# Two attention and two MLP layers on one core: a float32 first block, weights split in streaming slots, a rank for every operation, and four-tile attention steps

## The chip, the core and the metric

The kernel runs on one core of a Trainium2 chip. Its compute engines are PE (TensorE, matrix products), DVE (VectorE), ACT (ScalarE) and POOL (GpSimd); SP issues most of the transfers. The metric is the device time of one execution in microseconds, lower is better. Each number given for a kernel is the median of its runs.

## The reference

Four layers over 2048 tokens of 512 channels, in float32: attention, MLP mixer, attention, MLP mixer, each with layer norms and a residual.

```python
def _A_ref(x, wqkv, wo):            # H = 32 heads of Dh = 16; W, dil = 8, 2
    qkv = (x @ wqkv).reshape(B, S, 3, H, Dh)
    idx = pos[:, None] - off[None, :]                # off = arange(8) * 2
    logits = einsum("bhsd,bhswd->bhsw", q, k[idx]) * Dh ** -0.5
    attn = softmax(where(idx >= 0, logits, -1e9))
    o = einsum("bhsw,bhswd->bhsd", attn, v[idx])
    return o.reshape(B, S, D) @ wo

def _B_ref(x, w1, w2, w3, w4):
    h = gelu(layernorm(x) @ w1)                      # D x D
    # the four quarters of h's channels move by +1, -1, +2, -2 tokens
    x1 = x + shifted(h) @ w2
    return x1 + gelu(layernorm(x1) @ w3) @ w4        # 512 -> 1792 -> 512

x = x + _A_ref(layernorm(x), A_wqkv, A_wo)
x = x + _B_ref(layernorm(x), B_w1, B_w2, B_w3, B_w4)
x = x + _A_ref(layernorm(x), A_wqkv, A_wo)
x = x + _B_ref(layernorm(x), B_w1, B_w2, B_w3, B_w4)
```

## The kernel before

**Tiles and stages.** Tokens are cut into four blocks of 512, each block into four tiles of 128 tokens (one token per partition; even and odd tokens lie on the two halves of the partitions, so that the window's step of two is a step of one). Two layers of four blocks give eight passes n = 0 to 7. Each goes through five stages: `p1_stream(n)` (layer norm, transposes, q, K, V; `p1_quarters` for n = 0), `p2(n)` (attention, in four units of eight heads called quarters), `p3(n)` (wo, residual, norm, w1, gelu), `p4(n)` (shift, w2, residual, norm) and `p5(n)` (the MLP in 14 chunks of 128 hidden channels). Group n of `p4` and `p5` has three or four tiles, five in the last pass, because the shift needs the neighbouring block.

**Numbers.** A float32 operand is split into two float16 parts, hi and lo, after scaling by a power of two; a product is three float16 matmuls (`HLS`, hi*hi, hi*lo, lo*hi). So every weight goes through: load, sum of squares on ACT, a small matmul and a power on POOL that give the scale (`power_of`), hi on ACT, lo on DVE (`rest`). wqkv is split in two parts, q = 0 for the first quarter's columns and q = 1 for the others; `small_weight` does wo, w1 and w2; `big_pair(c)` takes two chunks of w3 and w4 at once through one of the large buffers nT or h, and writes the halves to DRAM (`w34_d`), from where `p5` reads them in every pass into the `w` places.

**Attention.** `p1_quarters` writes q, K and V of one quarter of block 0 straight into the q and kv places; eight transfers then shift K and V by one and two partitions, so that seven earlier tokens stand beside each. `p1_stream` writes q, K and V to DRAM, and each quarter of `p2` loads a window from there. A quarter works on two tiles at a time (`for i in (0, 2)`): multiply K by q (`prod`), sum over the head's 16 channels into `L`; then for all four tiles maximum, subtract, exp (ACT), sum, reciprocal, scale; then again two tiles at a time multiply V by the weights and add the eight window places in three additions. For n = 0 (`PE_SUMS = 1`) PE sums the products by 16 float32 matmuls with the identity per pair of tiles instead, which also transposes the result; `prod0` is a second product buffer for n = 0, which is afterwards lent out as two x and two f32 places (`LENT`).

**Order.** Nothing is emitted in the order of the code. `Graph` collects 3,000-odd operations with their buffers' cells; `plan` is a list scheduler that gives every engine, at each moment of an estimated time, the ready operation with the lowest key whose buffers have a free place, and so fixes each engine's order and each buffer's place. On the chip each engine runs its operations in that order and waits on semaphores. An operation's key is that of its stage, `n - 1.0` for p3 and so on, and `SHIFT` adds a correction by stage, pass and engine:

```python
key += sum(SHIFT.get(k, 0) for k in {(s, None, None), (s, None, e), (s, n, None), (s, n, e)})
```

The word "lock" marks DVE operations that the planner keeps apart from POOL's. Places: mm and acc (4 + 4 PSUM banks), x (9, later 11), f32 (6, later 8), kv (3), q, prod, L, o, ev, nT, h, g and w (8). At the start 64 matmuls on ones (`WARM`) run before any data has come.

## Time and profile before

| | |
|---|---|
| median of 3 runs | 1235.77 us (1235.09 to 1235.9) |
| the profiled execution, its own time | 1236.35 us |
| its span, first to last instruction | 1234.6 us |
| mean granted clock of PE | 0.983 |
| instructions | 16,935 |
| bytes moved by DMA | 175.22 MB, mean 142 GB/s |
| ACT table loads | 56, 71.8 us in all |

In the profile, L252 is the line of the helper that issues every instruction, so groups are told apart by their tiles: `out<-in`, numbers of buffers left out. A matmul row has the duration of one matmul from its first to its last cycle; matmuls overlap, so their cost to PE is the distance between their starts. In a view by time a row is a run of equal instructions with start, duration and count, and in brackets the idle time before it and what ended that. `SPq` rows are issues of transfers, and "granted clock" is the share of its full clock that PE had.

### The profile page before, as it was taken

How to read it: one execution, taken by the hardware profiler on the slowest of the kernel's cores; microseconds unless marked ns; L12 is line 12 of the kernel's file. 1: busy time of each engine (PE TensorE's matmuls, PEld its weight loads, DVE VectorE, ACT ScalarE, POOL GpSimd, SP SyncE). 2: the span in 40 equal slices, each digit the busy share in tenths (PEclk: the TensorE clock that was granted, in tenths of full speed). 3: DMA queues.
4: the chain of work that ended last, by engine and by line, in shares of the span. 5: the costliest groups of instructions: out<-in, count | busy, mean ns of one | idle time of the engine just before them, and what ended most of it. 6: DMA issues, size and time to landing. Idle time of an engine off the chain costs nothing.

```text
span 1234.6 us, 16935 instructions
## 1 busy us (share of the span) xinstructions
PE 1187.9 (96%) x6048; PEld 604.3 (49%) x6048; DVE 929.2 (75%) x1168; ACT 680.7 (55%) x1217; POOL 363.0 (29%) x512
## 2 busy tenths in 40 slices
PE   7799599999999999999999999999999999999997
PEld 5365364455454455444444445444444444444554
DVE  4787689988888999999887988798867898322011
ACT  6775566664655457545653656465556454344332
POOL 4230313412531146023621353135003441232100
PEclk9799799999999999999999999999999999999999
DMA  8546785576536543754347545743457344112321
GB/s 260 183 125 208 208 260 163 126 216 180 142 95 183 153 141 99 175 141 124 90 138 195 140 107 139 192 128 92 128 138 201 98 133 153 61 43 73 107 85 52
DMA packets 119556, 175.22 MB, mean 142 GB/s; under 512 B 11184, under 2 KB 61840, under 8 KB 119472
## 3 DMA queue, kind: packets, MB, share of 16 engines
q1 hardware_dynamic: 117440, 172.65, 49.6%
q10 hardware_dynamic: 2032, 1.50, 0.4%
q8 instruction: 47, 0.77, 0.3%
q14 instruction: 37, 0.30, 0.1%
HBM read 132.64 MB, written 37.87 MB: 138 GB/s over the span
## 4 chain that ended last, share of the span: by engine, by line
PE 85%; DMA 5%; ACT 4%; DVE 2%; SPq 1%; issue 1%; POOL 0%; DVEq 0%; ACTq 0%; POOLq 0%
PE mm L252 63%; PE acc L252 22%; DMA kv<-kv 2%; SPq L252 1%; DMA kv_d<-ev 1%; DVE L L252 1%; DMA w<-in_A_x_dram 1%; ACT g L252 1%; ACT junk L252 1%; DVE prod L252 1%; DMA h<-in_B_w_dram 0%; DMA nT<-in_B_w_dram 0%; DMA w<-g 0%; DMA q_d<-ev 0%; ACT kv L252 0%
## 5 line engine op out<-in xcount | busy, mean ns | idle before, releaser
L252 PE MATMUL acc<-w,g 128*128 128x512 f16 x1302 | 299.3, 379 | 0.0
L252 PE MATMUL mm<-nT,w 128*128 128x512 f16 (+1 forms) x1344 | 294.9, 373 | 0.0
L252 ACT ACTIVATE mm<-mm,s_w 128x512 f32<-128x512 f32 (+2 forms) x158 | 98.3, 623 | 253.3 <-PE mm L252 252.9
L252 PEld LDWEIGHTS <-g 128*128 128x128 f16 x1494 | 148.2, 99 | 167.3 <-issue 15.1
L252 PE MATMUL mm<-wq_hl,xt 128*128 128x512 f16 x1008 | 225.7, 379 | 0.4 <-ACT ev L252 0.3
L252 PEld LDWEIGHTS <-w 128*128 128x128 f16 x1512 | 141.0, 98 | 147.0
L252 DVE TENSOR_TENSOR prod<-kv,q 128x2048 f32<-128x2048 f32 x64 | 149.2, 2333 | 30.7 <-DMA kv<-kv 17.0
L252 PEld LDWEIGHTS <-xt 128*128 128x128 f16 x1008 | 98.6, 98 | 112.0 <-issue 0.7
L252 DVE TENSOR_TENSOR prod<-kv,L 128x2048 f32<-128x2048 f32 x64 | 148.8, 2330 | 0.9
L252 DVE TENSOR_REDUCE L<-prod 128x128 f32<-128x2048 f32 x64 | 145.7, 2279 | 0.6
L252 POOL TENSOR_TENSOR g<-f,g 128x512 f16<-128x512 f32 (+1 forms) x39 | 56.0, 1435 | 278.7 <-ACT f L252 271.6
L252 DVE TENSOR_TENSOR prod<-prod 128x1024 f32<-128x1024 f32 (+1 forms) x113 | 118.3, 1047 | 2.5
L252 PE MATMUL mm<-nT,w_hl 128*128 128x512 f16 x384 | 88.3, 379 | 0.4 <-ACT nT L252 0.2
L252 PE MATMUL mm<-wo_hl,oT 128*128 128x512 f16 x384 | 84.5, 379 | 0.0
L252 PE MATMUL mm<-w_hl,h 128*128 128x512 f16 x384 | 84.5, 379 | 0.0
L252 ACT ACT_TABLE_LOAD x56 | 71.8, 1283 | 19.1 <-PE mm L252 13.1
L252 DVE SCALAR_TENSOR_TENSOR g<-mm,c_g,g 128x512 f16<-128x512 f32 (+1 forms) x56 | 40.9, 729 | 48.7 <-ACT g L252 48.6
L252 ACT ACTIVATE g<-mm,c_g 128x512 f16<-128x512 f32 (+1 forms) x112 | 75.0, 672 | 3.3
L252 ACT ACTIVATE ev<-mm,s_kv 128x128 f32<-128x128 f32 x112 | 46.8, 470 | 54.1 <-PE mm L252 42.5
L252 POOL COPY h<-h 128x126 f16<-128x126 f16 (+3 forms) x56 | 43.1, 793 | 104.3 <-DVE h L252 101.5
L252 POOL TENSOR_TENSOR g<-prod,g 128x512 f16<-128x512 f32 (+1 forms) x17 | 25.4, 1496 | 151.8 <-ACT prod L252 151.8
L252 PEld LDWEIGHTS <-oT 128*128 128x128 f16 x426 | 41.6, 98 | 49.7
(183 smaller groups left out, 1424.9 us busy)
## 6 DMA issues: line engine op xcount, KB each, us to landing
w<-w SPq DMA_DIRECT2D x224, 256.0 KB
kv<-kv_d SPq DMA_DIRECT2D x112, 352.0 KB
kv_d<-ev SPq DMA_DIRECT2D x112, 128.0 KB
q_d<-ev SPq DMA_DIRECT2D x28, 256.0 KB
w<-g SPq DMA_DIRECT2D x28, 256.0 KB
q<-q_d SPq DMA_DIRECT2D x28, 256.0 KB
x<-x SPq DMA_DIRECT2D x27, 256.0 KB
w<-in_A_x_dram SPq DMA_DIRECT2D x32, 128.0 KB
```

What stands on the lines that cost most here:

```text
L252: i = f(*a, **k).ins
```

## The change

What it does, part by part:

- **Order.** `SHIFT` goes. `PLACES` gives each of the 3,029 operations, in the order in which the code makes them, a rank from 0 to 3,028, and that rank is its key.
- **Block 0 in float32.** `p1_quarters` turns the tiles into float32 (`turn_f32`) and multiplies them by the raw wqkv: four float32 matmuls of 384 columns per tile and quarter (for the first quarter 256 and 128). Quarters 1 to 3 are written to x places; from there one transfer each copies K and V into kv places, beside the shifts. In `p5(0)` (`PLAIN = 1`) w3 and w4 are loaded in float32 and used unsplit: per chunk 4 matmuls up, one gelu, 3 matmuls down. In the trace of before these were 12 and 9 in float16.
- **Splitting.** wqkv is split as a whole after block 0's products, with one scale; its evictions need one instruction instead of two. `hi` may go to ACT or POOL (`hi_of`), squares of wqkv to ACT or DVE. `big_pair` stages each of its four pieces in a `w` place. Loads of x of blocks 1 to 3 and of all weights but wqkv wait for the eviction of quarter 0's last q and K (`begun`).
- **Attention.** A quarter's four tiles go through the multiply, the sum over channels, the multiply by V and each addition in one instruction. `L` is laid out head, tile, window place, so that maxima and sums run over neighbours. `PE_SUMS` goes: block 0 adds on DVE and transposes like the others. `prod` is one buffer of four tiles; `prod0` and its lent places go (x 9, f32 6).
- **Norms.** The small instruction that made minus the mean goes; ACT's square takes the sum by its scale and bias.
- **Last pass.** In `p5(7)` all lo parts are made on DVE, and each part of a group has its own `down`.

```diff
-        key += sum(SHIFT.get(k, 0) for k in {(s, None, None), (s, None, e), (s, n, None), (s, n, e)})
-        o.key, o.alts, o.succ, o.n, o.est = key, alts, [], 0, 0.0
+        o.key, o.alts, o.succ, o.n, o.est = PLACES[len(self.ops)], alts, [], 0, 0.0
...
-        "x": places("x", X_OWN, [P, D], F32, const, part[:2]),
+        "x": places("x", 9, [P, D], F32),
-        "prod": places("prod", 1, [P, 2 * W * P], F32),
-        "prod0": places("prod0", 1, [P, 2 * W * P], F32),
+        "prod": places("prod", 1, [P, NT * W * P], F32),
-        "f32": places("f32", F_OWN, [P, D], F32, const, part[2:]),
+        "f32": places("f32", 6, [P, D], F32),
...
+    def turn_f32(key, n, dst, cell, out):
+
+        ps = Buf("mm")
+
+        def fn():
+            for c in range(NC):
+                f = slice(P * c, P * (c + 1))
+                T.transpose(ps.t[:, f], n.t[:, f], ident)
+        pe(key, 0.44, fn, [n], [ps, (dst, "new")])
+        act(key, 0.6, lambda: A.activation(out(), ps.t.rearrange("p (c t) -> p c t", c=NC), AF.Copy), [ps], cell)
...
+            q, kv = first_q[qt] = (Buf("x"), [Buf("x"), Buf("x")]) if qt else (Buf("q"), [Buf("kv"), Buf("kv")])
+            first = 0 if qt else PAD * P
...
+                for ks in ((0, 1), (2,)) if qt == 0 else ((0, 1, 2),):
...
+                        for c in range(NC):
+                            rhs = src_of(0, c) if f0 == 0 else src_of(1, c)[:, :, f0 - P:f0]
+                            T.matmul(o, f32v(xts[i].t, D)[:, P * c:P * (c + 1)], rhs[:, ks[0]:ks[0] + n],
+                                     start=(c == 0), stop=(c == NC - 1))
...
+                    if qt == 0 and i == NT - 1 and ks[0] == 0:
+                        begun = [done]
...
+                if qt:
+                    first_q["copied"] = dma(k1, lambda j=j, kv=kv: kv[j].t[:, PAD * P:], lambda j=j, src=src: src[j].t,
+                                        [(src[j], tiles)], [(kv[j], ("own", 0)), (kv[j], "new")], 0.8)
...
+        first = dve(kd + 0.05, 4.46, lambda pv4=pv4, q=q, kv=kv: V.tensor_tensor(
+            pv4(), win(kv[0].t, 0, NT),
+            q.t.rearrange("p (t f) -> p t f", t=NT).unsqueeze(2).to_broadcast([P, NT, W, P]), ALU.mult),
+            q_in + kv_in[0], [pr, (L, "new")], lock=True)
+        dve(kd + 0.04, 4.41, lambda pv4=pv4, Lv=Lv: V.tensor_reduce(
+            Lv(), pv4().rearrange("p t j (h d) -> p t j h d", d=DH), AX.X, ALU.add), [pr], [L])
...
+        dve(kd + 0.02, 4.46, lambda pv4=pv4, Lv=Lv, kv=kv: V.tensor_tensor(
+            pv4().rearrange("p t j (h d) -> p t j h d", d=DH), win_h(kv[1].t, 0, NT),
+            Lv().unsqueeze(4).to_broadcast([P, NT, W, H8, DH]), ALU.mult),
+            [all_L, *kv_in[1]], [pr, (o, "new")], lock=True)
...
-    VEC_G = (0, 2, 4, 6, 8, 10, 12)
+    PLAIN = 1
+    VEC_G = [2] * 7 + [1]
...
+        def up():
+            for k in range(NC):
+                T.matmul(ps.t[:, :P * K], f32v(w3.t, D)[:, P * k:P * (k + 1)],
+                         f32v(nT.t, NC * D)[:, D * k:D * k + P * K], start=(k == 0), stop=(k == NC - 1))
+
+        def down():
+            for k in range(K):
+                T.matmul(acc[k].t, f32v(g.t, D)[:, P * k:P * (k + 1)], f32v(w4.t, D),
+                         start=(c == 0), stop=(c == NF - 1))
...
-    p1_quarters()
     p2(0)
```

More of the change, by code (lines that the diff above doesn't have):

```diff
@@ L283, in __getitem__ @@
             return self.made[j]
-    X_OWN, F_OWN = 9, 6
-    part = [lambda j=j: slots["prod0"][0][:, D * j:D * (j + 1)] for j in range(4)]
-    LENT = [("x", X_OWN), ("x", X_OWN + 1), ("f32", F_OWN), ("f32", F_OWN + 1)]
     slots = {
@@ L491, in stage_of @@
         return (stage0, c) if q == 0 else (stage1[c // 2], c % 2)
-    ssq = [keep(f"ssq{q}", [P, NC]) for q in range(2)]
-    inv_q = [keep(f"inv_q{q}", [P, 1]) for q in range(2)]
     K0 = -9.0
@@ L640, in tile_mixer @@
[L640 removed]
+            [], [stage_of(1, c)], 1.9)
     SC = 3
@@ L834, in p1_stream @@
                                 "p (q f) -> p q f", q=4), [ev], [(kvb[l], qts(par, j - 1))], 0.6)
+    begun = p1_quarters()
+    for i in range(NT):
+        load_x(1, i, K0 + 1.0, begun)
+    op.stage = ("wqkv", 0)
+    ssq, inv_q = keep("ssq", [P, 2 * NC]), keep("inv_q", [P, 1])
+    for q in range(2):
+        for c in range(NC):
+            n = 3 * (P if q == 0 else D - P)
+            dst, acc = [lambda q=q, c=c: part(0, c, q).bitcast(BF16),
+                        lambda q=q, c=c: ssq.t[:, NC * q + c:NC * q + c + 1]]
+            op(-4.0, [(ACT, 0.3 + n * 0.00078, lambda q=q, c=c, dst=dst, acc=acc: A.activation(
+                dst(), src_of(q, c), AF.Square, accum_out=acc()), None),
+                      (DVE, 0.06 + n * 0.00137, lambda q=q, c=c, dst=dst, acc=acc: V.scalar_tensor_tensor(
+                dst(), src_of(q, c), 1.0, src_of(q, c), ALU.mult, ALU.mult, accum_out=acc()), "lock")],
+                [stage_of(q, c)], [(wq, (q, 0, c)), (ssq, (q, c))])
```

547 lines of the change are left out of this document (245 added, 302 removed), and 139 rows, old and new, of tables (PLACES, SHIFT).

## The prediction

> **What bounds the kernel now.** I read the busy shares first, then the span cut into stretches.
>
> ```profile
> PE 1187.9 (96%) x6048; PEld 604.3 (49%) x6048; DVE 929.2 (75%) x1168; ACT 680.7 (55%) x1217; POOL 363.0 (29%) x512
> ...
> 10.36:54.00 43.64, 29.02 (x137) 16.36 (x136) 26.91 (x55) 33.06 (x76) 7.85 (x17) 0.80 0.74 228
> 54.00:165.00 111.00, 90.97 (x556) 61.78 (x554) 83.84 (x117) 69.10 (x151) 28.93 (x38) 0.91 0.63 186
> 165.00:240.00 75.00, 71.64 (x365) 36.44 (x364) 68.66 (x100) 50.56 (x95) 26.06 (x36) 1.00 0.64 181
> 240.00:1200.00 960.00, 958.73 (x4769) 468.24 (x4768) 739.84 (x877) 515.06 (x874) 289.03 (x382) 1.00 0.48 132
> 1200.00:1234.60 34.60, 28.21 (x167) 14.01 (x165) 6.34 (x12) 9.39 (x18) 2.31 (x2) 0.95 0.17 57
> ```
>
> In a stretch the first number behind its bounds is its length, then busy PE, PEld, DVE, ACT, POOL, the granted clock and the DMA share. From 240 to 1200 us PE lacks 1.3 us: an edit there gains only if it takes work from PE. Length minus busy gives PE's gaps: 14.6, 20.0, 3.4, 1.3 and 6.4 us, of 46.7 in all (1234.6 - 1187.9); the first 10.36 us, mostly warm-up, have the other 1.0. The last 6.4 are output transfers; 38 us lie before 240, where the granted clock is 0.80 and 0.91 too. So I asked whom PE waited for (us in all, times, longest), and where (start, duration, count, in brackets the wait before).
>
> ```profile
> PE mm L252 <- ACT f L252: 14.0, 7, 7.8
> PE mm L252 <- DVE mx L252: 6.2, 1, 6.2
> ```
>
> ```profile
> 67.33 3.73 PE L252 MATMUL mm<-ident,prod 128*128 128x128 f32 x32
> 70.90 5.34 PE L252 MATMUL mm<-wq_hl,xt 128*128 128x512 f16 x24
> 76.08 2.11 PE L252 MATMUL mm<-wq_hl,g 128*128 128x384 f16 x12
> ...
> 79.73 2.11 PE L252 MATMUL mm<-wq_hl,g 128*128 128x384 f16 x12
> 81.68 0.60 PE L252 MATMUL mm<-ident,f 128*128 128x128 f32 x4
> 82.11 2.11 PE L252 MATMUL mm<-wq_hl,g 128*128 128x384 f16 x12
> ...
> 144.56 1.12 PE L252 MATMUL mm<-ident,f 128*128 128x128 f32 x4 [7.83 <-ACT f L252]
> ...
> 155.09 5.89 PE L252 MATMUL mm<-ident,prod 128*128 128x128 f32 x32 [6.16 <-DVE mx L252]
> ```
>
> The two largest gaps are bracketed. ACT, late at 144, had itself waited 9.6 us for a pair of MLP weights to land in its one big staging buffer; the gap at 155 is a power step of the same pairs:
>
> ```profile
> 141.93 1.06 ACT L252 ACTIVATE g<-h 128x1024 bf16<-128x1024 f32 x1 [9.62 <-DMA h<-in_B_w_dram]
> ```
>
> **The change part by part.** *PE's work.* Starts of groups give pitches: (76.08-70.90)/24 = 0.216 us for an f16 matmul of 512 columns, (81.68-79.73)/12 = 0.1625 for 384, (70.90-67.33)/32 = 0.1116 for one f32 record of 128, and 82.11-81.68 = 0.43 for four transposes. An f32 matmul leaves two records, so it costs 0.223 for 128 columns, which is four times an f16 column (0.1625 x 4/3 = 0.217). I price f32 at four f16 matmuls of its width: 0.65 for 384, 0.863 for 512; scaling the 128-column row gives 0.67 and 0.893 as the upper end.
>
> ```profile
> L252 PE MATMUL mm<-ident,prod 128*128 128x128 f32 x324 | 42.3, 285 | 7.3 <-DVE mx L252 6.2 <-ACT kv L252 1.1
> ```
>
> By the code, block 0's qkv has 16 x 12 = 192 f16 matmuls of 384 (31.2 us), which become 16 x 4 in f32 (41.6): +10.4. Its MLP up: 14 x 12 = 168 f16 (27.3) become 14 x 4 = 56 f32 (36.4): +9.1. Its down: 14 x 9 = 126 f16 of 512 (27.2) become 42 f32 (36.2): +9.0. Out go the 128 sums of products on PE (256 of the 324 records; the other 68 are transposes from lent places): -28.6. In come 16 transposes: +1.7. Net +1.6, at the upper f32 price +5.3. So PE gains no work and loses none: what the change is worth must come out of gaps and slow clock.
>
> *The beginning, 10 to 54 us.*
>
> ```profile
> 10.36 0.60 PE L252 MATMUL mm<-ident,f 128*128 128x128 f32 x4
> ...
> 11.29 0.58 ACT L252 ACTIVATE g<-mm 128x512 f16<-128x512 f32 x1
> ...
> 15.71 0.82 PE L252 MATMUL mm<-ident,f 128*128 128x128 f32 x4 [2.22 <-POOL f L252]
> 16.33 9.52 PE L252 MATMUL mm<-wq_hl,g 128*128 128x384 f16 x48
> ...
> 29.23 6.34 SPq L252 DMA_DIRECT2D kv<-kv  x8
> ...
> 31.74 7.61 DMA kv<-kv
> ```
>
> The first tile is turned at 10.36, but its products wait for the split of the weights until 16.33. In f32 they need only the turned copy (0.6 of ACT) and the raw weights: start near 12. Sixteen units of 2.6 us then run to about 54, because quarters 1 to 3 go to x places and no longer wait for the kv places that the attention holds. Row 52.60 below shows the streaming products starting at 52.6 already, so the split of wqkv, moved behind, is ready then if ACT and DVE keep their present pace. The gap of 14.6 should fall to 3; bounds 1 (ACT's copy alone) and 14.6. The split's squares and scalings stay on ACT, DVE and POOL, beside 42 us of PE work.
>
> ```profile
> 52.60 5.34 PE L252 MATMUL mm<-wq_hl,xt 128*128 128x512 f16 x24
> ```
>
> *Attention of block 0, 54 to 165 us.* Durations of one instruction on DVE:
>
> ```profile
> L252 DVE TENSOR_TENSOR prod<-kv,q 128x2048 f32<-128x2048 f32 x64 | 149.2, 2333 | 30.7 <-DMA kv<-kv 17.0 <-DMA kv<-kv_d 7.9 <-PE mm L252 5.5
> L252 DVE TENSOR_REDUCE L<-prod 128x128 f32<-128x2048 f32 x64 | 145.7, 2279 | 0.6
> L252 DVE TENSOR_TENSOR prod<-prod 128x1024 f32<-128x1024 f32 x56 | 74.4, 1329 | 0.6
> L252 DVE TENSOR_TENSOR prod<-prod 128x512 f32<-128x512 f32 x57 | 43.9, 771 | 1.9
> L252 DVE TENSOR_REDUCE mx<-L 128x32 f32<-128x256 f32 x64 | 39.0, 610 | 13.0 <-ACT L L252 12.6
> L252 DVE TENSOR_TENSOR L<-L,mx 128x256 f32<-128x256 f32 x64 | 29.2, 457 | 2.2
> L252 DVE TENSOR_TENSOR o<-prod 128x256 f32<-128x256 f32 x56 | 25.1, 449 | 1.9
> L252 DVE SCALAR_TENSOR_TENSOR g<-h,inv_p,g 128x512 f16<-128x512 f32 x16 | 11.1, 746 | 1.5 <-ACT g L252 1.5
> ```
>
> A quarter costs 2 x (2.333+2.333+2.279) + 2 x (1.329+0.771+0.449) + 2 x (0.610+0.457): 21.1 us. Four tiles at once double the width: from 1024 to 2048 columns the time grows by 1.004, so 4096 takes about 4.34 where two took 4.66; the three wide steps and three adds save some 1.7 us, 47 over the 28 quarters that already ran on DVE. The other layout of L I price at nothing, between -0.5 (contiguous maxima and sums) and +0.5 (scattered writes). Before 1200 this is under PE and earns nothing, as do the small scalings of the sums that go.
>
> For block 0, DVE's four quarters (4 x 19.4 = 78, the adds now included) start when the shifted K and V have landed. Landing took 7.61 us at 31.74 (a step of the chain of waits); quarter 0 is now done near 22, so 30. Beside them DVE splits wqkv (12 times 512 columns at 0.746: 9 us), wo, w1, w2 (9 more) and the turned tiles of the streams (12, 9 more): last output at 135, and with all 28 splits of the MLP weights in front (21) at 156. PE's work that needs no attention: 54 + 12 tiles x (36 x 0.216 + 0.43) = 152. So the gap here lies between 0 and 4 us for this chain alone; layer norms of block 0 without other work add a few. Of the present 20.0 us, 14.0 (7.83 + 6.16) hang on MLP weight pairs, which are first needed by block 1 now and stage in eight small w places. I take 8 left; bounds 0 and 20.
>
> *Slow clock.* Busy time by what the granted clock lacks is 29.0 x 0.20 + 91.0 x 0.09 = 14 us at most; directly, the 48 matmuls at 16.33 took 9.52 for 48 x 0.1625 = 7.8, the 32 records at 155.09 5.89 where those at 67.33 took 3.73. Fewer gaps, less of it: I take 8 of the 14 as gained, bounds 0 and 12. The Trainium skill, "TensorE: Matmul & The Clock Gate" (Part 1), says that an idle window of about 3.4 us halves the clock and as long a busy one restores it; the rows behind both long gaps agree (1.12 for 0.60 at 144.56, 5.89 for 3.73 at 155.09), and by that rule alone nearly all 14 would be gained, 6 us more than I take.
>
> *Places and order.* x and f32 lose two lent places each. 17 transposes used the f32 ones (68/4); were each delayed by one 0.75 us step, 13 us; I take 2 (PE has other work), bounds 0 and 13. The float32 MLP reads as many bytes as the split one. SP gets six more copies of K and V (0.8 us each by row 29.23), while PE works on streams. The loads of x of block 1, of wo, w1, w2 and of the MLP weights now wait for quarter 0's last q and K eviction near 22, and the shifts of K and V share their queue; the first user of that x is a stream near 54, 30 us later, against one landing of 7.6 us: nothing, and 7.6 once without that cover. `scale` steps, single evictions and the all-DVE last block shorten covered work: nothing.
>
> *Sum.* 1234.6 + 1.6 (PE) - 11.6 (beginning) - 12 (54 to 165) - 8 (clock) + 2 (places) = 1206.6 of span. Around it lay 1236.35 - 1234.6 = 1.75 us; the profiled execution was 0.6 above the median of 1235.77. So 1207.7; I say 1207.
>
> **The rivals.** *A: everything fills.* Gaps at their lower bounds (1, 0), clock 12, no cost of places: 1234.6+1.6-13.6-20-12+1.2 = 1192. For it: 152 us of independent work against 135. Against: a static order meets late transfers.
>
> *B: DVE's chain decides block 0.* All MLP splits come first and the K and V transfers slip by 8 us in each of three quarters: output at 156 + 24 = 180 against 152, a gap of 28 instead of 8: 1228. For it, DVE's 17 us of waits on kv<-kv; against, three kv places let a pair load ahead.
>
> *C: the longer lock, slower than before.*
>
> ```profile
> 64.94 2.29 DVE L252 TENSOR_TENSOR prod<-kv,q 128x2048 f32<-128x2048 f32 x1 [1.25 <-PE mm L252]
> 65.49 1.80 POOL L252 TENSOR_SCALAR a<-a 128x1 f32<-128x1 f32 x1 [1.16 <-ACT junk L252]
> 68.37 0.19 POOL L252 TENSOR_SCALAR a<-a 128x1 f32<-128x1 f32 x1
> 68.64 0.55 POOL L252 TENSOR_TENSOR a<-a,nhalf 128x1 f32<-128x1 f32 x1
> ...
> 69.29 0.26 POOL L252 TENSOR_SCALAR a<-a,a 128x1 f32<-128x1 f32 x1
> ...
> L252 POOL TENSOR_TENSOR a<-a,nhalf 128x1 f32<-128x1 f32 x32 | 25.0, 782 | 3.2 <-DVE a L252 0.8
> L252 POOL TENSOR_SCALAR a<-a,a 128x1 f32<-128x1 f32 x32 | 21.2, 664 | 3.2
> ```
>
> POOL's 0.19 us step at 65.49 ends only with DVE's multiply. With a multiply of 4.4 us such a wait doubles, about +0.64 us for each of 96 layer norm chains (the last two steps take 0.782 + 0.664 in the mean and 0.55 + 0.26 undisturbed): 61 us if PE stood still for each, 1269; more than 44 of 96 must be exposed to lose what I forecast. If six in ten are, 1245. Against it: PE lacks 1.3 us in 960. The Trainium skill, "SBUF — State Buffer" (SBUF: two separate sides), states this lock for a DVE operation with two SBUF inputs against a GpSimd one that reads SBUF, for the whole instruction; the row agrees.
>
> *D: the change does not do what it says.* The table gives only precedence among ready operations; if the real order of transfers leaves PE as idle as before, 1234.6 + 1.6 + 2 - 2 + 1.2: 1237.
>
> **How the numbers follow.** Forecast 0.52 (1198 to 1217), A 0.14, B 0.18, C 0.10, D 0.06. About 0.2% (2.5 us) is what a measurement of this kernel can tell from no change. The range 1190 to 1233 holds forecast, A and B; C and D lie above. Faster: 0.52+0.14+0.18 and a little of D, 0.85; same: 0.05; slower: C, 0.10.
>
> **What would show it.** The first qkv matmul near 12 and the streams near 54; PE busy about 1181 with the same steady stretch; DVE multiplies of 4.35 us; gaps before 240 near 14. Wrong would be: a PE gap over 10 us, between 100 and 200 us, before wo (B); gaps after 240 released by POOL or ACT f (C); an f32 pitch of 512 above 0.9 us.

## The result, and the profile after

The changed kernel takes 1240.79 us (median of 8 runs, 1238.06 to 1245.12), the kernel before 1235.84 beside it (8 runs, 1234.47 to 1239.03): ratio 1.0039, 95% interval 1.0022 to 1.0057. It is slower by 0.4%; forecast was 1207. The profiled execution took 1240.41 us, its span is 1238.3.

The busy line of the page and the same stretches as before (length, then busy PE, PEld, DVE, ACT, POOL, granted clock, DMA share, GB/s):

```profile
PE 1193.5 (96%) x5676; PEld 592.2 (48%) x5676; DVE 903.5 (73%) x896; ACT 632.0 (51%) x1108; POOL 372.4 (30%) x516
```

```profile
10.36:54.00 43.64, 40.75 (x179) 27.84 (x178) 25.60 (x33) 26.73 (x77) 19.20 (x24) 1.00 0.61 194
54.00:165.00 111.00, 88.69 (x385) 41.62 (x384) 88.75 (x88) 57.75 (x119) 25.90 (x37) 0.91 0.65 174
165.00:240.00 75.00, 69.83 (x322) 35.32 (x320) 70.70 (x80) 50.64 (x94) 31.23 (x44) 0.95 0.69 198
240.00:1200.00 960.00, 951.15 (x4542) 463.26 (x4540) 707.24 (x676) 486.37 (x798) 287.47 (x374) 1.00 0.49 135
1200.00:1238.30 38.30, 33.78 (x201) 16.86 (x198) 7.48 (x13) 7.60 (x16) 0.00 (x0) 0.97 0.23 69
```

Length minus busy gives PE's gaps, to set beside those of the prediction. The prediction gave its 2 us for lost places no stretch; the forecast column has them in the steady one, from 240 to 1200. The last column is a kernel found in the experiments (e11_wide_between); most of its rows are shown there.

| us | before | forecast | after | e11 |
|---|---|---|---|---|
| gap 10.36 to 54 | 14.6 | 3 | 2.9 | 1.5 |
| gap 54 to 165 | 20.0 | 8 | 22.3 | 12.1 |
| gap 165 to 240 | 3.4 | 3.4 | 5.2 | 5.8 |
| gap 240 to 1200 | 1.3 | 3.3 | 8.9 | 1.1 |
| gap after 1200 | 6.4 | 6.4 | 4.5 | 4.5 |
| PE busy | 1187.9 | 1181.5 | 1193.5 | 1186.6 |
| span | 1234.6 | 1206.6 | 1238.3 | 1212.6 |

The opening gained its 11.7 us. The rest of the table took them back: +2.3 from 54 to 165, +1.8 up to 240, +7.6 in the steady stretch, +5.6 of PE's busy time, -1.9 at the end. Together +3.7. The traces split the 5.6: PE was busy for 22.0 us under a granted clock of 0.50 before and for 27.5 us after. Counting half of such time as lost gives 11.0 and 13.7 us, so 2.7 are clock and the other 2.9 work; e11, with the same matmuls, has 8.1 and thus 1.6 of work, as forecast. The rows of PE by time (start, duration, count, in brackets the wait before):

```profile
12.21 1.16 PE L358 MATMUL mm<-nT,g 128*128 128x128 f32 x8 [0.69 <-ACT g L358]
...
53.76 10.52 PE L358 MATMUL mm<-wq_hl,xt 128*128 128x512 f16 x48
...
87.69 5.03 PE L358 MATMUL mm<-wq_hl,xt 128*128 128x512 f16 x12 [4.22 <-ACT ev L358]
...
137.98 1.12 PE L358 MATMUL mm<-ident,f 128*128 128x128 f32 x4 [4.77 <-ACT f L358]
...
172.87 2.75 PE L358 MATMUL mm<-wo_hl,oT 128*128 128x512 f16 x12
...
241.35 2.74 PE L358 MATMUL acc<-w,g 128*128 128x512 f32 x6
243.92 2.74 PE L358 MATMUL mm<-nT,w 128*128 128x384 f32 x8
246.50 0.60 PE L358 MATMUL mm<-ident,o 128*128 128x128 f32 x4
```

The first float32 product starts at 12.21 and the streams at 53.76, as forecast; 2.57/3 = 0.857 and 2.58/4 = 0.645 us bear out the float32 prices of 0.863 and 0.65. But the row at 87.69 waits 4.22 us for an eviction of ACT and takes 5.03 us where 12 matmuls of the same width take 2.75 at 172.87. ACT stood as well. Two of its rows, and the issue of SP that the second waited for:

```profile
76.30 0.69 ACT L358 ACTIVATE ev<-mm,s_q 128x512 f32<-128x512 f32 x1 [5.97 <-DMA kv_d<-ev]
...
86.34 0.63 ACT L358 ACTIVATE junk<-w 128x512 bf16<-128x512 f32 x1 [7.20 <-DMA w<-in_B_w_dram]
```

```profile
80.55 0.73 SPq L358 DMA_DIRECT2D w<-in_B_w_dram  x1
```

The piece for which ACT stands from 79 on is issued at 80.55. And the sums of PE's waits (us, times, longest), where before ACT's f led with 14.0:

```profile
PE mm L358 <- ACT ev L358: 16.5, 8, 4.2
PE mm L358 <- ACT f L358: 16.0, 9, 4.8
```

So transfers were late; the first question was whether SP issued them late, whether they landed late, or whether something else (the 4.4 us steps of DVE) held everything.

### The profile page after: what moved, and what is told of

It is laid out like the page before. It is cut to its first block, busy times and chain, and to the rows that moved or that the text cites. A ratio compares the mean times of both kernels' runs of the same rounds, so it can differ in the third digit from the quotient of the medians.

```text
span 1238.3 us, 15802 instructions
## 1 busy us (share of the span) xinstructions
PE 1193.5 (96%) x5676; PEld 592.2 (48%) x5676; DVE 903.5 (73%) x896; ACT 632.0 (51%) x1108; POOL 372.4 (30%) x516
## 4 chain that ended last, share of the span: by engine, by line
PE 76%; DVE 7%; DMA 7%; ACT 3%; POOL 2%; SPq 2%; issue 2%; ACTq 0%; DVEq 0%; POOLq 0%
PE mm L358 54%; PE acc L358 22%; DVE prod L358 3%; SPq L358 2%; DMA kv<-kv_d 2%; DMA kv<-x 1%; DVE L L358 1%; POOL b L358 1%; DMA w<-in_A_x_dram 1%; POOL a L358 1%; DMA h<-in_B_w_dram 1%; ACT junk L358 1%; DMA q<-q_d 1%; ACT ev L358 1%; DMA kv_d<-ev 1%
## 5 line engine op out<-in xcount | busy, mean ns | idle before, releaser
L358 PE MATMUL acc<-w,g 128*128 128x512 f16 (+1 forms) x1260 | 309.0, 394 | 0.0
L358 ACT ACTIVATE mm<-mm,s_w 128x512 f32<-128x512 f32 (+1 forms) x144 | 90.6, 629 | 228.8 <-PE mm L358 228.5
L358 DVE TENSOR_TENSOR prod<-kv,q 128x4096 f32<-128x4096 f32 x29 | 128.6, 4434 | 20.2 <-DMA kv<-kv_d 12.2
L358 DVE TENSOR_TENSOR prod<-kv,L 128x4096 f32<-128x4096 f32 x32 | 141.4, 4418 | 0.6 <-DMA kv<-kv_d 0.3
L358 DVE TENSOR_REDUCE L<-prod 128x256 f32<-128x4096 f32 x32 | 141.2, 4414 | 0.1
L358 DVE TENSOR_TENSOR prod<-prod 128x2048 f32<-128x2048 f32 x64 | 117.5, 1837 | 1.1
L358 POOL TENSOR_TENSOR g<-f,g 128x512 f16<-128x512 f32 x42 | 61.0, 1453 | 189.7 <-ACT g L358 89.4
L358 PE MATMUL mm<-ident,f 128*128 128x128 f32 x384 | 59.0, 280 | 21.0 <-ACT f L358 16.0
L358 ACT ACTIVATE g<-mm,c_g 128x512 f16<-128x512 f32 x98 | 66.9, 685 | 2.1
L358 PEld LDWEIGHTS mm<-ident,f 128*128 128x128 f32 x384 | 47.2, 143 | 40.2 <-ACT f L358 19.1
```

Of the source, the lines that this page charges most:

```text
L358: i = f(*a, **k).ins
```

## The experiments

All of them keep the changed kernel's order on every engine (e7 that of before) except where a text says so. "Gap" is PE's, in the stretch named. Each ratio is to the kernel before on the same chip.

### Is it PE, the pieces of weights, or the length of DVE's steps?

**e4_slack.** Ten us of PE's work in front of the streams:

```diff
+                    for _ in range(94 * (n == 1 and i == j == 0)):
+                        T.matmul(ps.t[:, :2 * P], warm[:, :P], warm, start=True, stop=True)
```

> The changed kernel in its own order; 94 matmuls of 256 columns on ones, about 10 us of PE at full clock, stand in front of one of the first streaming products, near 54 us. They change no other engine's work. If PE's time is what counts (every us of PE is a us of the whole), the time rises by 10: 1251. Theory T (ACT, DVE and the transfers set the pace up to 110 us, and PE stands behind them): most of it is taken up by the gaps that follow, +0 to +4: 1241 to 1245, with the gap from 54 to 165 us at 12 to 18 us instead of 22 and the first product of wo near 173 to 177. This would mean that the 11.7 us that the opening gained were worth little by themselves.

Measured: 1239.81 us, 1.0038 [1.0025, 1.0051]: the ten us are free. Its rows:

```profile
54.00:75.00 21.00, 20.22 (x139) 13.64 (x139) 16.10 (x10) 11.64 (x28) 3.01 (x9) 1.00 0.29 85
75.00:100.00 25.00, 22.08 (x105) 11.87 (x104) 16.71 (x18) 11.72 (x24) 8.31 (x8) 1.00 0.77 199
100.00:165.00 65.00, 54.20 (x237) 24.62 (x237) 55.62 (x60) 34.88 (x68) 10.16 (x20) 0.89 0.72 193
```

The gap from 54 to 165 is 14.5 us instead of 22.3 (111 less the three busy times), so 7.8 of the ten us went into it, and the clock granted from 75 to 100 is 1.00: over the whole trace PE loses 11.9 us to the half clock instead of 13.7. Whatever sets the pace up to 165 us, it isn't PE: the 11.7 us of the opening could be spent again without loss.

**e3_squares.** ACT does not wait for the pieces of w3 and w4 in their 28 squares:

```diff
-                junk, v(), AF.Square, accum_out=ss_p[c].t[:, m:m + 1]), [t], [(ss_p[c], m)])
+                junk.rearrange("p (a f) -> p a f", a=4), ones.unsqueeze(1).to_broadcast([P, 4, P]),
+                AF.Square, accum_out=ss_p[c].t[:, m:m + 1]), [t], [(ss_p[c], m)])
```

> The changed kernel in its own order; the 28 sums of squares over pieces of w3 and w4 read a tile of ones instead of the piece, so ACT does not wait there for a piece to land (the scale of these pieces is then another power of two; the first reader of a piece is its hi part). Theory T with ACT as the one that is held (19.3 us of ACT's waits are for such pieces, 7.2 us of it at 79 to 86 us): PE's waits for ACT's evictions between 75 and 100 us fall from 8 to 3 us, the gap from 54 to 165 us to 14 to 18 us, the time by 3 to 8 us: 1233 to 1238. If DVE's chain of block 0 or the shifted K and V decide, the waits only move: 1239 to 1242.

Measured: 1241.33 us, 1.0047 [1.0032, 1.0062], no gain. The next late transfer takes the wait over: ACT waits 9.54 us for the load of h (`h<-in_B_w_dram`) at 92.69, and PE 7.98 us for ACT behind it.

**e1_halves.** Each four-tile step as two instructions of two tiles, back to back (the multiply shown; the others alike):

```diff
-        first = dve(kd + 0.05, 4.46, lambda pv4=pv4, q=q, kv=kv: V.tensor_tensor(
-            pv4(), win(kv[0].t, 0, NT),
+        first = dve(kd + 0.05, 4.46, lambda pv4=pv4, q=q, kv=kv: [V.tensor_tensor(
+            pv4()[:, i:i + 2], win(kv[0].t, i, 2),
...
+            for i in (0, 2)],
```

> The changed kernel in its own order; each four-tile step of attention (multiply by q, sum over channels, multiply by the weights, the three additions) is issued as two instructions of two tiles, back to back. DVE gets about 0.2 us per split step: 96 more instructions, some 12 us, under PE's work. Theory T (transfers issued late by SP hold ACT and DVE between 47 and 110 us, and the gaps follow): the gap from 54 to 165 us stays at 20 to 25 us; only the POOL steps of norms that wait for a 4.4 us multiply (two of the three later breaks of PE, at 829 and 960 us, have such a step of 4.29 and 4.55 us in their chain of waits) get shorter, so 0 to -4 us against the changed kernel's 1240.8: 1237 to 1241. Rival C (the longer lock is what eats the gain): the gaps after 240 us fall from 8.8 to about 2 and the gap from 54 to 165 us by 5 or more, 1225 to 1232.

Measured: 1242.41 us, 1.0054 [1.0039, 1.007]. The gap after 240 us stays at 8.1. This seemed to clear the long steps, but a row of POOL shows that nothing was shortened:

```profile
822.34 4.27 POOL L358 TENSOR_SCALAR b<-b,b 128x1 f32<-128x1 f32 x1
```

The step of one element a partition waits out both multiplies of 2.2 us; in the changed kernel it took 4.28 us at that place. Two instructions back to back hold DVE's queue and POOL as long as one. The test was no test of the length, and I came back to it with e10 and e11.

### Transfers that run on one or two DMA engines

**e2_merged.** Two shifts of K or V, on the two halves of the partitions, become one over all 128:

```diff
-                        dma(k1 + 0.01, lambda ...: kv[j].t[64 * par + d:64 * par + 64, s0 * P:(s0 + n_) * P], ...
+                        to = P if qt else 64 * par + 64
+                        dma(k1 + 0.01, lambda ...: kv[j].t[64 * par + d:to, s0 * P:(s0 + n_) * P], ...
```

> The changed kernel in its own order; for quarters 1 to 3 of block 0 the two transfers that shift K (or V) by one or two partitions on the two halves of the partitions become one over all 128 (what crosses the middle falls on window places that the mask removes), so 12 of SP's issues go, 0.6 to 0.9 us each, between 41 and 112 us. Theory T: SP issues without a pause from 58 to 88 us, and the pieces of MLP weights and of w1 for which ACT then waits 7.2 and 3.5 us are issued 4 to 8 us sooner; the gap from 54 to 165 us falls from 22 to 13 to 18 us, and the time by 3 to 8 us: 1233 to 1238. Rival R (landing, that is bandwidth or latency, is what is late, not issue): gap and time as in the changed kernel, 1239 to 1242. Rival C: the same as R.

Measured: 1273.7 us, 1.0306 [1.0293, 1.0319]: fewer issues, and 33 us slower than the changed kernel. No expectation had that. The rate of all DMA engines from 42 to 58 us, in 40 slices of 0.4 us (the first line in tenths of the engines' time), and one of SP's issues:

```profile
DMA  9996862121110000077576679676866310000000
GB/s 362 372 370 238 239 216 91 72 74 61 67 49 27 26 26 26 26 266 266 147 210 182 233 268 280 200 236 205 246 205 200 113 41 20 26 26 26 20 26 24
```

```profile
72.92 9.88 SPq L358 DMA_DIRECT2D kv_d<-x  x1
```

The rate falls to 26 GB/s twice, for 2 us from 47 on and for 3 us from 55 on; 254 KB (127 partitions of 2 KB) at 26 GB/s are 10.0 us. An issue of a transfer of 4 KB took 9.88 us. In the changed kernel the same view from 56 to 76 us, in slices of 0.5 us, has plateaus at 45 to 50, twice that, where its shifts of 62 partitions run (their rows of 1,536 bytes are 35 of 63 and 58 of 83 packets in the two plateaus):

```profile
DMA  1111255441111111000002596421144312789999
GB/s 47 49 48 49 71 143 116 127 159 72 50 49 45 47 49 49 26 23 12 8 16 61 188 360 205 152 89 32 46 82 123 115 39 82 172 191 229 205 234 205
```

The engines' share of time is below one tenth at 26 GB/s and one tenth at 50, which fits one engine of 16 for 127 partitions and two for 62. The Trainium skill, "DMA: Bandwidth & Descriptors" (Why a DMA increments its semaphore by 16 and not by 1), says that a transfer issued by SP or ACT uses the largest number of engines up to 16 that divides the size of the slowest dimension on both sides, and that they are the lowest-numbered ones. By that rule 127 gives 1, 62 gives 2, 63 gives 9. Both plateaus agree with 1 and 2; which engines they are no run here shows. That made theory K (a transfer runs on as many engines as divide its number of partitions) and the next three kernels. Its rival I is that the number of SP's issues decides.

**e5_split62.** A shift of 62 partitions as 48 and 14:

```diff
+                            for a, z in ((d, 64),) if d == 1 else ((d, d + 48), (d + 48, 64)):
+                                q.dma_start(kv[j].t[64 * par + a:64 * par + z, s0 * P:(s0 + n_) * P], ...
```

> Theory K, formed after e2_merged: a transfer is spread over as many of the 16 DMA engines as divide its number of partitions. In e2_merged the rate stood at 25 GB/s for 10 us after each shift of 127 partitions, in the changed kernel at 45 to 50 GB/s around the shifts of 62 (and its DMA share at one tenth): one engine and two. All that is issued behind such a shift waits for these two engines. Here the changed kernel in its own order issues each shift of 62 partitions (16 of them, 93 KB) as two, of 48 and 14 partitions; the shifts of 63 (9 engines) stay. SP gets 14 more issues, 9 us. Theory K: 93 KB take 0.3 us on 14 to 16 engines instead of 1.9 on two, 30 us of two engines in all; the gap from 54 to 165 us falls from 22 to 8 to 14 us, the time to 1226 to 1235. Rival I (the rate of SP's issues decides): 14 issues more make it slower, 1243 to 1250.

**e6_wide.** Three shifts for K or V of a quarter instead of four, of 126, 112 and 15 partitions:

```diff
+                        rows_of = {(0, 1): (16, P), (1, 1): (1, 16), (0, 2): (2, P)}.get((par, d))
...
+                                a, z = rows_of
+                                q.dma_start(kv[j].t[a:z, s0 * P:(s0 + n_) * P],
+                                            src[j].t[a - d:z - d, first + (NT - n_) * P:first + NT * P])
```

> The changed kernel in its own order; block 0's four shifts of K (or V) per quarter become three: one of 126 partitions by two (14 engines by theory K), one of 112 (16) and one of 15 (15) by one; what crosses the middle of the partitions falls on window places that the mask removes. 4 issues fewer on SP and 4 fewer on ACT than in the changed kernel. Theory K: as e5_split62 without its added issues, and the shifts of 63 (9 engines) gain too: the gap from 54 to 165 us at 6 to 12 us, the time 1222 to 1233. Rival I: with 4 of SP's issues fewer 1237 to 1240. Where the order itself is what holds PE (the DVE chain of block 0): 1238 to 1242 in both.

**e7_wide_before.** The same in the kernel before:

```diff
-                        dma(key - 1.0, lambda ...: kv[j].t[64 * par + d:64 * par + 64, s0 * P:(s0 + n_) * P], ...
+                                Y.dma_start(kv[j].t[a:z, s0 * P:(s0 + n_) * P],
+                                            kv[j].t[a - d:z - d, (NSL - n_) * P:NSL * P])
```

> The kernel before in its own order, with the shifts of block 0 as in e6_wide (24 issues instead of 32). It has as many shifts of 62 partitions (16), so by theory K it stands behind them as well. If the changed kernel suffers more from them because its order counts on them earlier (copies into the kv places, x and pieces of weights queued behind them), the kernel before gains less than the changed one, 0 to -5 us: 1231 to 1236, and e6_wide is the faster of the two. If both gain alike, the shifts explain the lateness, but not why the change brought nothing.

**e16_nine** (a later run): e6_wide with the shift by one as two of 63 partitions:

```diff
-                        rows_of = {(0, 1): (16, P), (1, 1): (1, 16), (0, 2): (2, P)}.get((par, d))
+                        rows_of = {(0, 1): (1, 64), (1, 1): (65, P), (0, 2): (2, P)}.get((par, d))
```

> e6_wide in its own order and with as many issues; only the shift by one partition goes again as two transfers of 63 partitions (9 engines by theory K) instead of one of 112 (16) and one of 15 (15). e5_split62 (62 cut into 48 and 14, the shifts of 63 kept, 5 or 6 issues for K or V of a quarter) reached 1233.8 us with a gap of 20.0 us from 54 to 165, e6_wide (3 issues) 1222.9 with 12.0. If the 11 us between them are the 16 shifts of 63 on 9 engines (126 KB, 0.56 us on nine at 25 GB/s each, against 0.31 on 16): 1229 to 1234. If they are SP's issues (theory I in part): 1221 to 1225.

Measured: e5 1233.8 us (0.998 [0.9966, 0.9995]), e6 1222.92 (0.9901 [0.9884, 0.9918]), e7 1221.67 (0.9882 [0.9864, 0.9899]), e16 1223.72 (0.9905 [0.9888, 0.9923]). The stretches of e6_wide, then of e7_wide_before:

```profile
10.36:54.00 43.64, 41.80 (x184) 28.48 (x182) 32.38 (x37) 28.12 (x82) 17.23 (x29) 1.00 0.66 212
54.00:165.00 111.00, 98.96 (x452) 47.62 (x451) 98.39 (x106) 63.76 (x128) 26.66 (x39) 0.94 0.73 196
...
240.00:1200.00 960.00, 950.81 (x4590) 463.13 (x4589) 696.15 (x670) 487.75 (x801) 289.39 (x374) 1.00 0.48 132
```

```profile
10.36:54.00 43.64, 29.69 (x144) 16.63 (x143) 27.37 (x56) 33.26 (x77) 8.28 (x19) 0.84 0.82 237
54.00:165.00 111.00, 102.07 (x623) 68.36 (x622) 95.31 (x130) 79.02 (x166) 30.17 (x37) 0.95 0.75 217
...
240.00:1200.00 960.00, 958.36 (x4770) 467.49 (x4768) 729.11 (x869) 509.80 (x867) 288.59 (x382) 1.00 0.47 130
```

Theory K holds: the gap from 54 to 165 falls from 22.3 to 12.0, and in the kernel before from 20.0 to 8.9. It isn't engines alone. e5, with 14 issues of SP more than the changed kernel, gained only 7 us and kept a gap of 20.0; e16, with e6's number of issues and nine engines for two of its three shifts, is as fast as e6. So nine engines are enough, and the 11 us between e5 and e6 go with the number of issues, 20 of SP and 4 of ACT: rival I is right for that part. e6 and e16 also have 6 issues of SP and 2 of ACT fewer than the changed kernel (not 4 and 4, as expected), e7 8 of SP fewer than its own; at 11 us for 20 issues that is an estimated 3 to 4 us of their gain, and no run widened the shifts at the same number of issues. And e7 says what K does not explain: both kernels gain 14 to 18 us, so the narrow shifts explain why transfers were late, not why the change brought nothing. With them gone the changed kernel still loses 3.1 us from 54 to 165 and 7.6 after 240 to the kernel before.

### The length of DVE's steps

**e10_wide_inter and e9_wide_places.** Multiply, sum, multiply, sum, two tiles at a time and nothing between; e9 also gives the lent places back:

```diff
+            for i in (0, 2):
+                p = pv4()[:, 0:2]
+                V.tensor_tensor(p, win(kv[0].t, i, 2), ..., ALU.mult)
+                V.tensor_reduce(Lv()[:, i:i + 2], p.rearrange("p t j (h d) -> p t j h d", d=DH), AX.X, ALU.add)
...
-        dve(kd + 0.04, 4.41, lambda pv4=pv4, Lv=Lv: V.tensor_reduce(
+        dve(kd + 0.04, 4.41, lambda: None, [pr], [L])
```

```diff
+    more = {'x': 11, 'f32': 8}
```

> e6_wide in its own order; each attention step goes as before the change, two tiles at a time: multiply, sum over channels, multiply, sum; then multiply, three additions, multiply, three additions, in a product buffer of two tiles (DVE +0.2 us per split step, 7 of them a quarter, 45 us in all, under PE's work). In e1_halves the two multiplies stood back to back, and POOL's small steps still waited 4.27 and 3.95 us for both together; here the sum over channels comes between them. Rival C (the lock of 4.4 us makes the later gaps): from 240 to 1200 us 8.6 falls to 3 to 5 us, the time from 1222.9 to 1217 to 1220. If the order makes them, 1222 to 1226, slower where DVE's chain of block 0 (1.5 us more a quarter) decides.

> e10_wide_inter with the two x and two f32 places that the change took away given back (in the 8 KB that the smaller product buffer leaves): the same order on every engine, places given out anew by the longest free. Theory L (the later gaps, 8.6 us from 240 to 1200 us in e6_wide against 1.6 in the kernel before with the same shifts, come from the lost places): they fall to 2 to 3 us against e10_wide_inter, the time by 5 to 7 us. If they come from the order, 0 to -1 us against e10_wide_inter.

Measured: e10 1347.49 us (1.0904 [1.088, 1.0929]), e9 1348.03 (1.0907 [1.0882, 1.0932]). Both are 125 us slower than e6, outside everything expected. (The gap of e6_wide after 240 us is 9.2, 960 - 950.81, not 8.6 as the two expectations have it.) DVE's rows of e10 show why:

```profile
256.24 2.29 DVE L358 TENSOR_TENSOR prod<-kv,q 128x2048 f32<-128x2048 f32 x1
258.56 2.29 DVE L358 TENSOR_REDUCE L<-prod 128x128 f32<-128x2048 f32 x1
260.89 2.29 DVE L358 TENSOR_TENSOR prod<-kv,q 128x2048 f32<-128x2048 f32 x1
263.21 2.29 DVE L358 TENSOR_REDUCE L<-prod 128x128 f32<-128x2048 f32 x1
265.42 0.74 DVE L358 SCALAR_TENSOR_TENSOR oT<-mm,c_o,oT 128x512 f16<-128x512 f32 x1
```

In e6_wide's order evictions stand between the multiply and the sum. Here one of them waits 9.2 us, and PE with it (20.2 us of PE's waits are for `DVE nT` alone, 0.9 in the changed kernel). So the time in which DVE's queue lets nothing else through has a price of its own: 2.3 us before the change, 4.4 after, 9.2 here. e9 against e10 shows nothing for the places, but in a kernel whose PE lacks 78 us after 240, so it says little about them.

In the changed kernel itself the longest wait after 240 us begins on POOL, at 820 us, in rows of DVE, POOL, ACT and PE:

```profile
820.61 4.42 DVE L358 TENSOR_TENSOR prod<-kv,L 128x4096 f32<-128x4096 f32 x1
```

```profile
820.87 4.28 POOL L358 TENSOR_SCALAR b<-b,b 128x1 f32<-128x1 f32 x1
```

```profile
825.19 0.81 ACT L358 ACTIVATE f<-x,b,b 128x512 f32<-128x512 f32 x1 [4.80 <-POOL b L358]
...
828.60 0.68 ACT L358 ACTIVATE ev<-mm,s_q 128x512 f32<-128x512 f32 x1
```

```profile
829.33 0.89 PE L358 MATMUL mm<-ident,f 128*128 128x128 f32 x4 [2.79 <-ACT ev L358]
```

POOL's step of one element a partition ends with DVE's multiply, ACT's norm waits for POOL, its later eviction comes late by that, and PE waits for the eviction. The second longest wait is of the same kind, behind a multiply that starts at 954.32:

```profile
954.33 4.54 POOL L358 TENSOR_SCALAR b<-b,b 128x1 f32<-128x1 f32 x1
```

```profile
959.77 1.12 PE L358 MATMUL mm<-ident,f 128*128 128x128 f32 x4 [2.60 <-ACT f L358]
```

These two are 5.4 of the 8.9 us. The third, 1.80 us at 461.26, stands behind residual additions that DVE takes up after a 4.42 us multiply at 447.63, and behind a POOL step of 2.39 us.

**e11_wide_between.** Halves again, and what DVE has next, if it is independent and counted on to be ready, goes between them (done while the instructions are emitted):

```diff
+            elif o.eng == DVE:
+                if o.est <= t0 + d * k and not hasattr(o.fn, "parts"):
+                    o.fn()
+                    rest_.pop(0)()
...
+        if hasattr(o.fn, "parts"):
+            ps = o.fn.parts()
+            ps[0]()
+            held = (o, ps[1:], t, o.alts[0][1] / len(ps), 1)
```

> e6_wide with the four-tile steps cut in two again, and DVE instructions that stand next in DVE's own order, need nothing of the step and were counted on to be ready by then, let through between the halves; every other engine keeps its order. e10_wide_inter did the opposite: two steps in one stretch of 9 us with nothing between them, and PE waited for DVE's evictions everywhere (1347 against 1223). Theory H (an instruction of 4.4 us holds DVE's evictions and POOL's small steps twice as long as one of 2.3; that is what the change pays for its four-tile steps): the gaps from 240 to 1200 us fall from 9.2 to 2 to 5 us, those from 54 to 165 us from 12.0 to 8 to 11 us, the time from 1222.9 to 1213 to 1219. If the order and not the length of the steps makes the later gaps: 1221 to 1226.

**e13_between.** The same without the wide shifts, so only the steps' length is undone in the changed kernel, with DVE's next work let in between:

> The changed kernel with its narrow shifts as they are, and only the DVE steps cut in two with other DVE instructions let through between the halves (as in e11_wide_between). Theory H: the gaps from 240 to 1200 us fall from 8.9 to 1 to 3 us and the time by 6 to 9 us, from 1240.8 to 1232 to 1235, which is 1 to 4 us under the kernel before: without its four-tile steps the rest of the change would have been a small gain. If the length of the steps only counts once the shifts are spread: 1238 to 1242.

Measured: e11 1214.45 us, 0.9831 [0.9816, 0.9846]; e13 1232.63, 0.9963 [0.9944, 0.9982]. The stretches of e11_wide_between, then of e13_between:

```profile
54.00:165.00 111.00, 98.90 (x450) 47.21 (x449) 99.61 (x127) 63.92 (x128) 24.48 (x37) 0.94 0.72 193
165.00:240.00 75.00, 69.23 (x289) 35.65 (x288) 67.65 (x83) 46.53 (x86) 29.83 (x41) 0.95 0.71 209
240.00:1200.00 960.00, 958.93 (x4653) 468.05 (x4652) 714.38 (x828) 489.04 (x804) 262.67 (x374) 1.00 0.48 132
```

```profile
54.00:165.00 111.00, 86.31 (x373) 40.21 (x371) 88.20 (x105) 57.81 (x119) 23.61 (x37) 0.91 0.62 166
...
240.00:1200.00 960.00, 959.42 (x4607) 468.81 (x4606) 726.17 (x837) 489.57 (x806) 258.02 (x375) 1.00 0.49 136
```

From 240 to 1200 us the gap falls from 9.2 (e6) to 1.1, and from 8.9 (after) to 0.6, though DVE has more work (921.6 us in e11 against 904.1 in e6). POOL's step at the place of the one at 820.87 now waits out one half:

```profile
802.50 2.43 POOL L363 TENSOR_SCALAR b<-b,b 128x1 f32<-128x1 f32 x1
```

From 54 to 165 us nothing is gained: 12.1 against 12.0 in e11, 24.7 against 22.3 in e13. Theory H (a step of 4.4 us holds DVE's evictions and POOL's small steps twice as long as one of 2.3) holds, and adds to K: undoing the long steps alone turns the change from 0.4% slower to 0.4% faster.

### What is left between 54 and 165 us

**e8_wide_squares** (e6 with the squares of e3), **e12_wide_short** (e6 with block 0's wide steps done for one tile of four, the three others left out), **e14_wide_between_xpool** (e11 with x of blocks 2 and 3 issued by POOL) and **e15_both_waits** (e14 with the squares of e3). The edits of e12 and e14:

```diff
+        nt = NT if n else 1
...
-            pv4(), win(kv[0].t, 0, NT),
+            pv4()[:, :nt], win(kv[0].t, 0, nt),
```

```diff
-                Y.dma_start(out(par), in_(par))
+                q.dma_start(out(par), in_(par))
...
+             G if b >= 2 else Y)
```

> e6_wide in its own order, with the 28 sums of squares over pieces of w3 and w4 reading a tile of ones (as in e3_squares). With the shifts spread, the profile of e6_wide still has 12.0 us of PE's gap from 54 to 165 us; 3.2 us of ACT's waits before the gap of 4.8 us at 121 are for such a piece, in front of the squares of three layer norms. Theory T' (what is left of that gap is ACT held by the pieces that the change moved into the w places): 12 falls to 7 to 9 us, the time from 1222.9 to 1217 to 1220. If what is left is the order itself (a pile of squares, power steps and DVE's 4.4 us steps): 1222 to 1224.

> e6_wide in its own order, with the wide steps of block 0's attention (multiply, sum, multiply, three additions) done for one tile of four; the three other tiles are left out, so DVE has some 52 us less between 40 and 165 us (the layout of L and o is as before, the rest of them zeros). Rival B of the prediction (DVE's chain decides block 0: in e6_wide DVE is busy 98 of the 111 us from 54 to 165): the gap from 54 to 165 us falls from 12.0 to 3 to 7 us, the first product of wo comes well before 157 us, the time falls by 5 to 12 us. If ACT's and the transfers' waits keep PE: gap 9 to 13 us, time 0 to -4 us.

> e11_wide_between with the 16 loads of x of blocks 2 and 3 (two of them the halves of a tile each) issued by POOL instead of SP, at the same place in the whole order. In e11_wide_between 12.1 us of PE's gap from 54 to 165 us are left; in e8_wide_squares ACT's wait before the gap of 4 us at 122 went from a piece of weights to a tile of x, whose load stood in SP's queue behind stores of q, K and V that themselves waited for ACT's evictions. Theory S (the rest of the gap is SP's queue: ACT waits for x, x for SP, SP for ACT): 12.1 falls to 6 to 9 us, the time from 1214.5 to 1208 to 1212. If the x tiles wait for their place and not for the queue, or POOL's own queue holds them as long (it waits for ACT's squares 14 to 17 us at a time there): 1213 to 1220.

> e14_wide_between_xpool with, besides, the 28 sums of squares over pieces of w3 and w4 reading a tile of ones (as in e3_squares). Each of the two edits alone moved ACT's wait before the gap near 121 us to the other kind of load: with ones instead of pieces it waited 3.05 us for a tile of x, with x issued by POOL 5.29 us for a piece of weights (and PE 6.40). Theory W (the two loads share the eight w places and one queue of ACT, and cover for each other): with both waits gone the gap from 54 to 165 us falls from 13.9 to 6 to 9 us, the time from 1215.5 to 1207 to 1212. If the order or DVE sets the rest: 11 to 14 us, 1213 to 1217.

Measured: e8 1223.7 us (0.9899 [0.9874, 0.9924]), e12 1224.17 (0.9896 [0.9883, 0.991]), e14 1215.46 (0.9818 [0.9796, 0.9839]), e15 1213.79 (0.9799 [0.9776, 0.9823]). None moves the time from that of its base, so the gains that the four expectations put first did not come. The stretch in e12_wide_short, then in e15_both_waits:

```profile
54.00:165.00 111.00, 101.00 (x466) 48.74 (x465) 61.19 (x103) 65.83 (x134) 19.52 (x40) 0.95 0.75 202
```

```profile
54.00:165.00 111.00, 99.16 (x464) 48.21 (x463) 102.03 (x130) 65.48 (x132) 30.71 (x49) 0.97 0.74 196
```

With DVE relieved of 37 us the gap is still 10.0, and with both kinds of waits of ACT taken away 11.8. So it is mainly neither DVE's chain of block 0 nor one kind of load. In all four PE waits 3.9 to 6.4 us between 115 and 123 us for a layer norm of ACT; in e8 that norm stands behind six squares in a row. That these 12 us are the order itself is what is left, but no run shows it: another order was not tried.

## Why the prediction was wrong

**The opening** (-11.6 us) was right: 11.7, with the start at 12.21 and the streams at 53.76. So were the float32 prices (0.857 and 0.645 against 0.863 and 0.65) and DVE's four-tile instructions, 4.42 and 4.43 us in the mean against 4.34 forecast:

```profile
L358 DVE TENSOR_TENSOR prod<-kv,L 128x4096 f32<-128x4096 f32 x32 | 141.4, 4418 | 0.6 <-DMA kv<-kv_d 0.3 <-DMA kv_d<-x 0.2
...
L358 DVE TENSOR_TENSOR prod<-kv,q 128x4096 f32<-128x4096 f32 x29 | 128.6, 4434 | 20.2 <-DMA kv<-kv_d 12.2 <-DMA kv<-kv 4.5 <-DMA q<-q_d 3.5
```

DVE is 25.7 us less busy, and as forecast this earned nothing.

**The gap from 54 to 165 us** (20.0 to 8, -12 us) is the first step that failed; it went to 22.3. The step read two waits, 7.83 and 6.16 us, as the work of the pairs of MLP weights, and held that moving the pairs behind smaller places would end them. e7_wide_before leaves the pairs where they were and widens the shifts: of the two waits only the second is left, the wait of 7.83 is gone:

```profile
140.79 6.66 PE L252 MATMUL mm<-ident,prod 128*128 128x128 f32 x32 [6.36 <-DVE mx L252]
```

That one was a late transfer, and transfers were late for another reason: shifts on two engines, and a queue of SP without a pause. The change kept the shifts and added six copies to that queue, which the prediction priced at nothing because PE would be at the streams; but ACT waits for what that queue brings, and PE for ACT's evictions. What the six copies cost by themselves no run shows. The trace of before says so too, in a view that the prediction didn't use, the rate of the DMA engines from 28 to 48 us in slices of 0.5 us, with its plateau at 44 to 50 GB/s behind the eight shifts that start at 29.23 (from 40 to 41 us every packet has 1,536 bytes, the row of a shift of 62 partitions):

```profile
GB/s 172 270 90 295 397 406 299 344 397 279 193 161 173 171 79 133 136 103 46 46 50 44 49 49 49 46 99 209 52 49 62 222 214 123 45 12 16 221 184 217
```

What the change does to this gap with the shifts out of the way is 12.0 against 8.9, a loss of 3. The cause of that rest stays open.

**The steady stretch** (+2 us for lost places) is the second: +7.6. Its cause is not shown to be the places; it is the four-tile steps, which the prediction weighed as rival C and priced through the lock alone. C's mechanism is there, and its sign too, gaps after 240 us released by ACT's f: 5.4 of the 8.9 us follow POOL steps of 4.28 and 4.54 us. The rest and e10 show a second price, DVE's own queue, with evictions and residual additions behind a step of 4.4 us; e11 and e13 undo both at once, so no run divides the two. The size of both together by e13 against the changed kernel is 1.0039 - 0.9963 = 0.76%, 9.4 us, a quarter of the 38 us of C's 1245. My count was too high, and my reason against it ("PE lacks 1.3 us in 960") wrong: that was true of steps of 2.3 us.

**The slow clock** (-8 us) is the third, and hangs on the first two. The loss rose by 2.7 us, because long gaps moved rather than went. By stretch, half of PE's busy time at a granted clock of 0.50 went from 7.1 to 0 us in the opening, but from 3.9 to 8.0 us from 54 to 165, from 0 to 2.8 up to 240 and from 0 to 3.0 in the steady stretch. The row at 87.69 is a case, 5.03 us for 2.75 behind a gap of 4.22. In e11, with the gaps down, the loss is 8.1 us. The 14 us that the prediction had as the most were too many as well: it spread the missing clock evenly over busy and idle time, and the trace of before has 11.0.

**The rivals.** D's sentence, that late transfers leave PE as idle as before, was closest (1237 against 1240.8; it had 0.06). B's sign, one PE gap over 10 us before wo, did not come: 11.7 us lie between 100 and 165, in waits of at most 4.8. Its mechanism did not hold either: e12 takes 37 us from DVE there and gains nothing. The first product of wo came at 172.87, 0.7 us later than before. The sum failed less by any price than by its form: it took an opening's gain as time when nothing had shown that PE set the pace behind it. e4_slack puts 10 us of matmuls there for nothing.

**What is fastest.** Both hindrances removed, the change is worth having: 1214.45 us (e11) against 1221.67 for the kernel before with wide shifts alone (e7); against the kernel before, measured beside each, the ratios are 0.9831 and 0.9882, and their intervals do not meet.

## What to carry to other kernels

A gain in an opening is a gain only if PE sets the pace behind it; put ten us of idle matmuls there and see whether they cost anything before counting on it. Look at the rate of the DMA engines in narrow slices when a transfer lands late: here plateaus at 26 and 45 to 50 GB/s were transfers that fit one and two engines, and the cure was the number of partitions, not the number of bytes. In a kernel with a fixed order the longest stretch in which one engine's queue lets nothing through is a price of its own: doubling an instruction saves 0.2 us a time on DVE and makes its neighbours wait up to 2 us more.

## What the runs showed of the hardware that was not expected

A transfer between partitions of SBUF moved at 26 GB/s with 127 partitions and at 45 to 50 with 62, while the shifts of 126, 112 and 63 showed no such plateau; and an issue of 4 KB behind such transfers took 9.88 us on SP's queue, where the changed kernel's issues of such stores take 0.2 to 0.8. Why it took so long no run shows.

Two DVE multiplies back to back kept a one-element step of POOL waiting 4.27 us, through both; it did not slip in between. The Trainium skill, "SBUF — State Buffer" (SBUF: two separate sides), states the lock for the whole of one instruction; for two in a row the row of e1_halves is what there is.
